# Six more weight blocks prepared during attention, the hash bits first in a score tile, and the instruction order computed anew

## The chip, the cores and the metric

One core of a Trainium2 chip runs the whole program. The metric is the device time of one execution in microseconds (us). The engines are TensorE (PE, with its weight loads as PEld), VectorE (DVE), ScalarE (ACT), GpSimd (POOL) and SyncE (SP), which issues nearly all transfers.

## The reference

Attention with a hash mask, then a gated feed-forward layer:

```python
q_bits = (einsum('bhsd,dk->bhsk', q, proj) > 0)          # 6 bits for each query; k_bits likewise
mask   = q_bucket[:, :, :, None] == k_bucket[:, :, None, :]
scores = where(mask, q @ k.T / sqrt(64), -1e9)           # 4 batches, 8 heads, 768 x 768, head size 64
attn   = exp(scores - max) ; attn /= attn.sum + 1e-9
x      = (attn @ v) as 3072 tokens x 512
out    = (sigmoid(x @ w_gate) * (x @ w_val)) @ w_out     # 512 -> 1536 -> 512
```

The three weight matrices come as 64-bit floats.

## The kernel before

Attention runs over 16 pairs of heads (4 batches, 4 pairs each); a pair has two query groups of three tiles. For a pair, k and q are loaded, turned on PE (tiles `tk`, `tq`), split into a high and a low part (`kh`, `kl`, `qh`, `ql`; every float32 product is three reduced products: low by high, high by low, high by high), and hashed (`hk`, `hq`, with the hash weights `hw`), which gives the bits `kb` and `qb` in bfloat16. `qs..` are q's parts with its halves exchanged by a transfer.

A score tile (`scores`, L713 to L727; 192 of them) is one accumulation of eight matmuls that run in pairs on the upper and lower 64 rows of the array: three pairs of float32 parts (L720) and, last, one bfloat16 pair that adds the hash match (L725). DVE takes the scores out of PSUM with their maximum (L734, `e`), ACT exponentiates (L753), PE turns `e` back in chunks (`tp`, L786), ACT or DVE copies a chunk out (`ef`, L793), and PE multiplies with v (`pv`, L803).

The feed-forward layer has 12 column blocks j. Each block of each matrix (`g`, `v`, `o`: 36 in all) must be made from 64-bit words (`load_w`, L297 to L375): a 512 KB load `raw`, then on DVE `exponent` (L321), `mantissa` (L328), `whole` (L333) and `signed` (L338), on ACT `shifted` (L324) and `high` (L351), on POOL `scaled` (L343) and `low` (L354). There are three classes of blocks. The j below `J1 = 3` are made during attention and stay. The j from 3 to 7 (`J2 = 8`) are made during attention, stored to DRAM (`kept`) and fetched back when attention's buffers are gone (the "switch"). The j from 8 to 11 are loaded and made after the switch, beside the feed-forward work. For six of the eight token units (384 tokens each) the j below 3 are worked off during attention too (`moe_early`: `zg`, `zv`, `zo`); the rest is the late stage (`moe_late`, names ending in `l`), where PE goes through gate (`zg`, 12 matmuls), value (`zv`, 12) and output (`yo`, 9) block by block. Gate products wait in one of two PSUM banks until ACT has made the sigmoid (`sig`, L579).

All instructions are first recorded as tasks. A planner (`Plan.order`) walks through them with written-down durations and buffers and emits them in the order in which its own clock starts them; every engine executes its part strictly in that order. So the written numbers set the order, not the time. `BEGIN` and `LEAVE` are what it charges when PE changes its kind of work, `PATIENCE` how long it puts off a change. A task that two engines could do is listed for both; the second takes it only by a key raised by `SECOND`. A transfer is held to land 2 us plus a share for its bytes after its issue (`dma`, L288). The matmuls `idle` (L273) are stand-ins without use that keep PE at work before data is there.

Of the kernel before, what the change touches and what calls it, by code (L numbers as in the profile page):

```python
# [9 lines left out]
F32 = mybir.dt.float32  # L10
F32R = mybir.dt.float32r
# [8 lines left out]
P = 128  # L20
# [10 lines left out]
SECOND = 3  # L31
# [5 lines left out]
BEGIN = dict(scores=95, turn=36, values=0, all=0)  # L37

PATIENCE = dict(rows=6000, columns=1000, all=1500)
# [130 lines left out]
def lsh_attention_glu_kernel(ctx, tc, q, k, v, proj, w_gate, w_val, w_out, out):  # L170
    nc = tc.nc
# [12 lines left out]
    J2 = 8  # L184
# [22 lines left out]
    praw = const.tile([P, NB], F32, name="praw")  # L207
    nc.scalar.dma_start(praw[0:D], proj)
    nc.scalar.dma_start(praw[D : 2 * D], proj)
# [31 lines left out]
    ALL = range(P // HB)  # L241
    for n, signs, groups in (("q", (1.0, -1.0), ALL), ("k0", (-1.0, 1.0), ALL[::2]), ("k1", (-1.0, 1.0), ALL[1::2])):
        w = const.tile([P, P], F32, name=f"hw{n}", tag="hw")
        nc.vector.memset(w, 0.0)
        for g in groups:
            half = g % 2 if n == "q" else g // 2
            rows = slice(half * D, (half + 1) * D)
            for i, sign in enumerate(signs):
                at_ = g * HB + i * NB
                nc.vector.tensor_scalar_mul(w[rows, at_ : at_ + NB], praw[rows], sign)  # L250
        hi, lo = hw[n] = [const.tile([P, P], F32R, name=f"hw{n}{x}") for x in "hl"]
        nc.scalar.copy(hi, w)
        nc.vector.tensor_sub(lo, w, f(hi))
# [18 lines left out]
    def busy():  # L272
        nc.tensor.matmul(idle, zero[:, :P], zero, start=True, stop=True)  # L273

    W_KEY, W_STEP, W_MORE = 12.0, 2.2, 1.6
    stock = dict(
        one=1, two=3, moe=1, z=2, y=4, kr=2, qr=2, vr=2, h=2, e=12, st=3, su=3, sv=2, rb=2, xs=3,
# [8 lines left out]
    FIRST = -1  # L286

# [9 lines left out]
    def load_w(key, n, j, early, last=None):  # L297
# [69 lines left out]
        c1 = add(key, "dve", 340, mantissa, after=[b1])  # L367
        c2 = add(key, "dve", 610, whole, after=[c1])
        d = add(key, "dve", 610, signed, after=[b2, c2], give=["raw2" if last else "raw1"])
        e = add(key, "pool", 1230, lambda: scaled(nc.gpsimd), after=[d])  # L370
        h = add(key, "act", 520, high, after=[e], take=[] if early or last else ["wk"])
        made[n, j] = add(key, "pool", 1230, lambda: low(nc.gpsimd), after=[h], give=["mid2" if last else "mid1"])
# [231 lines left out]
    def pair(i):  # L604
# [6 lines left out]
        def load(n):  # L611

            if n == "k":
                z[n] = at.tile([P, 2, GT, 2, D], F32, name=f"kr{u}", tag="kr", bufs=stock["kr"])
                from_ = k[b, two].rearrange("h (p c) d -> p h c d", c=NC)
                for h in range(2):
                    for j in range(2):
                        nc.sync.dma_start(z[n][:, h, :, j], from_[:, h, j * GT : (j + 1) * GT])
            else:
                z[n] = at.tile([P, NC, 2, D], F32, name=f"qr{u}", tag="qr", bufs=stock["qr"])  # L620
                from_ = q[b, two].rearrange("h (p c) d -> p h c d", c=NC)
                for m in range(2):
                    nc.sync.dma_start(z[n][:, :, m], from_[:, m])
# [49 lines left out]
        def bits_k(h):  # L673
# [5 lines left out]
            n: add(t0 - 10.72, "sp", 2400, lambda n=n: load(n), tail=4000, take=[n + "r"]) for n in "kq"  # L679
        }  # L680
        needs, last_turn = [], None
        for m, n in enumerate("kq"):
            n_ = t0 - 6 + m
# [8 lines left out]
        for m, n in enumerate("kq"):  # L692
            n_ = t0 - 2.8 + m * 0.6
            a = add(n_, "pe", 6 * MM, lambda n=n: hash_(n), after=[needs[m]], take=["two"])
# [12 lines left out]
    def group(i, g, z, needs, v_here):  # L707
# [162 lines left out]
    for m, (n, j) in enumerate(order):  # L870
        load_w(W_KEY + W_STEP * m + W_MORE * max(0, m - 3 * J1), n, j, j < J1)
# [60 lines left out]
```

## Time and profile before

| what | value |
|---|---|
| median of 3 runs | 1087.22 us (1086.17 to 1087.38) |
| the profiled execution | 1087.43 us |
| its span, first to last instruction | 1085.6 us |
| PE busy | 1057.6 us, 97% of the span |
| DVE, ACT, POOL busy | 569.8, 488.2, 260.6 us |
| TensorE clock granted, mean over the span | 0.997 |

The profile covers one execution. Busy time is the sum of an engine's instructions; a matmul's end is modelled, so PE can be slower than it could be while it counts as busy. Times in timelines count from the start of the span. Attention reaches to about 566 us, the late stage from there to the end. The profiled execution lies 0.2 us from the median, and what is outside its span is 1.8 us.

### The profile page before, as it was taken

The page shows a single profiled execution, that of the slowest core. Times are in us where ns is not written, and L with a number is a line of the kernel's source. Part 1 is how long each engine was busy: PE and PEld are TensorE (multiplying, and loading weights), DVE is VectorE, ACT ScalarE, POOL GpSimd, SP SyncE. Part 2 cuts the span into 40 slices and gives each one's busy share as a digit, 9 for nine tenths or more (in the row PEclk, how much of TensorE's full clock was granted, in tenths as well). Part 3 has the DMA queues.
Part 4 walks back from the last instruction along what each step waited for, and adds up shares of the span by engine and source line. Part 5 has one row for each costly group of instructions (what it writes and reads, how often), then busy time and mean ns, then how long its engine had stood idle before and what let it go on. Part 6 is the DMA issues. An engine that isn't in the chain of part 4 may idle for free.

```text
span 1085.6 us, 20467 instructions
## 1 busy us (share of the span) xinstructions
PE 1057.6 (97%) x8409; PEld 847.1 (78%) x8412; DVE 569.8 (52%) x1200; ACT 488.2 (45%) x878; POOL 260.6 (24%) x235
## 2 busy tenths in 40 slices
PE   9999999999999999999997999999999999999998
PEld 5665567677676776776676889999999999999997
DVE  6899989778778677788730881001120202020201
ACT  2766777667686667775641342112121212121211
POOL 0013243212323122322021672112121212121211
PEclk9999999999999999999999999999999999999999
DMA  8345464444555346424129321002020202020010
GB/s 204 83 130 156 128 180 127 140 119 134 179 142 166 110 128 192 143 70 148 47 83 356 113 82 59 1 1 88 1 88 1 88 1 88 1 74 14 29 30 30
DMA packets 109117, 107.24 MB, mean 99 GB/s; under 512 B 60128, under 2 KB 91872, under 8 KB 109024
## 3 DMA queue, kind: packets, MB, share of 16 engines
q1 hardware_dynamic: 108864, 105.93, 31.7%
q8 instruction: 66, 1.08, 0.4%
q14 instruction: 27, 0.22, 0.1%
q10 hardware_dynamic: 160, 0.00, 0.0%
HBM read 67.64 MB, written 25.69 MB: 86 GB/s over the span
## 4 chain that ended last, share of the span: by engine, by line
PE 79%; DVE 10%; POOL 5%; issue 2%; DMA 2%; ACT 2%; POOLq 0%; DVEq 0%; ACTq 0%
PE pv L803 10%; PE sc L720 8%; PE zv_1l L427 7%; PE zg_1l L427 7%; PE yo_1l L460 7%; PE tp L786 6%; PE zv_0l L427 6%; PE zg_0l L427 5%; PE yo_0l L460 5%; PE zg L427 4%; PE zo L460 3%; PE zv L427 3%; DVE e L734 3%; PE sc L725 2%; PE hk L658 2%
## 5 line engine op out<-in xcount | busy, mean ns | idle before, releaser
L753 ACT ACTIVATE e<-e,st 128x768 f32<-128x768 f32 x192 | 196.3, 1025 | 90.4 <-DVE st L746 90.2
L734 DVE TENSOR_SCALAR_CACHE_REDUCE e<-sc 128x768 f32<-128x768 f32 x192 | 177.8, 952 | 32.0 <-PE sc L725 30.9
L803 PE MATMUL pv<-ef,vr 128*64 128x384 f32 x768 | 140.9, 496 | 0.0
L443 DVE TENSOR_TENSOR gf_1l<-zv_1l,sig 128x384 f32<-128x384 f32 x39 | 21.7, 557 | 208.6 <-PE zv_1l L427 208.6
L786 PEld LDWEIGHTS tp<-ident,e 64*128 64x128 f32 x2304 | 84.7, 139 | 33.2 <-issue 18.5
L793 DVE COPY ef<-tp 128x768 f32<-128x768 f32 x96 | 90.9, 952 | 35.4 <-PE tp L786 33.6
L443 DVE TENSOR_TENSOR gf_0l<-zv_0l,sig 128x384 f32<-128x384 f32 x39 | 21.6, 555 | 162.8 <-PE zv_0l L427 162.8
L786 PE MATMUL tp<-ident,e 64*128 64x64 f32 x2304 | 95.6, 226 | 4.3 <-DVE e L734 1.6
L427 PE MATMUL zg_0l<-xh_0l,wg 128*128 128x384 f32 x312 | 88.1, 342 | 7.3 <-ACT sig L579 7.2
L720 PE MATMUL sc<-kh,ql 64*128 64x384 f32 x192 | 85.9, 447 | 4.8 <-DVE ql L648 2.6
L803 PEld LDWEIGHTS pv<-ef,vr 128*64 128x64 f32 x768 | 48.3, 136 | 52.2 <-issue 48.0
L813 POOL TENSOR_TENSOR xs<-xs,rb 128x384 f32<-128x384 f32 x32 | 32.8, 1025 | 233.8 <-DVE xs L810 174.8
L427 PE MATMUL zv_0l<-xh_0l,wv 128*128 128x384 f32 x312 | 85.9, 336 | 2.5 <-DVE gf_0l L443 2.5
L793 ACT COPY ef<-tp 128x768 f32<-128x768 f32 x96 | 75.1, 793 | 25.9 <-PE tp L786 25.5
L720 PE MATMUL sc<-kh,qsl 64*128 64x384 f32 x192 | 85.9, 448 | 0.8 <-DVE ef L793 0.6
L427 PE MATMUL zg_1l<-xh_1l,wg 128*128 128x384 f32 x312 | 86.4, 337 | 0.0
L427 PE MATMUL zv_1l<-xh_1l,wv 128*128 128x384 f32 x312 | 85.5, 334 | 0.0
L448 POOL TENSOR_TENSOR gl<-gf_1l,gh 128x384 fp32r<-128x384 f32 x39 | 40.5, 1040 | 184.4 <-ACT gh L447 184.4
L460 PE MATMUL yo_0l<-wo,gh 128*128 128x512 f32 x234 | 73.5, 395 | 0.0
L460 PE MATMUL yo_1l<-wo,gh 128*128 128x512 f32 x234 | 73.4, 395 | 0.0
L579 ACT ACTIVATE sig<-zg_1l 128x384 f32<-128x384 f32 x39 | 19.2, 492 | 116.0 <-PE zg_1l L427 116.0
L448 POOL TENSOR_TENSOR gl<-gf_0l,gh 128x384 fp32r<-128x384 f32 x34 | 37.0, 1089 | 135.1 <-ACT gh L447 135.0
(160 smaller groups left out, 2506.7 us busy)
## 6 DMA issues: line engine op xcount, KB each, us to landing
kr<-in_k_dram SPq DMA_DIRECT2D x64, 96.0 KB
qr<-in_q_dram SPq DMA_DIRECT2D x32, 192.0 KB
vr<-in_v_dram SPq DMA_DIRECT2D x16, 384.0 KB
qsh<-qh SPq DMA_DIRECT2D x32, 192.0 KB
qsl<-ql SPq DMA_DIRECT2D x32, 192.0 KB
rb<-rd SPq DMA_DIRECT2D x64, 96.0 KB
xd<-xs SPq DMA_DIRECT2D x32, 192.0 KB
rawg<-in_moe_w_gate_dram SPq DMA_DIRECT2D x12, 512.0 KB
```

What stands on the lines that cost most here:

```text
L427: nc.tensor.matmul(z["acc"][:, :GN], a[:, wc], x[xx][:, c, :], start=(c == 0 and i == 0), stop=(c == KC - 1 and i == 2),)
L443: nc.vector.tensor_mul(z["gf"], z["acc"][:, :GN], sig[:, j])
L448: low = lambda eng: eng.tensor_sub(gl[:, j], z["gf"], f(gh[:, j]))
L460: nc.tensor.matmul(acc, a[:, slot, ts_], w, start=(first and i == 0), stop=(last and i == 2))
L658: nc.tensor.matmul(acc[:, j, :GN], hw[w][a], z[n + x][:, j * GN : (j + 1) * GN], start=m == 0, stop=m == 2,)
L720: nc.tensor.matmul(sc[:, j, :GN], q_[rows, c], z["k" + x][rows, h * GN : (h + 1) * GN], start=(m == 0), stop=False, tile_position=(j * D, 0),)
L734: nc.vector.tensor_scalar(sp(e), gz["sc", t, h][:, :, :GN], -SCALE, None, op0=ALU.mult, op1=ALU.min, accum_out=gz["st", t][:, 0, h : h + 1],)
L753: nc.scalar.activation(e, e, AF.Exp, bias=st[:, 2, h : h + 1], scale=st[:, 1, h : h + 1], accum_out=gz["su"][:, h * GT + t : h * GT + t + 1],)
L786: nc.tensor.transpose(tp[:, r, at_ : at_ + D], gz["e", t, h][rows, c * P : (c + 1) * P], ident[rows, rows], tile_position=(r * D, 0),)
L793: copy(gz["ef", c].rearrange("p (n r d) -> p r n d", r=2, d=D), gz["tp", c][:, :, :GN].rearrange("p r (n d) -> p r n d", d=D),)
L803: nc.tensor.matmul(gz["pv"][rows, :GN], z["v"][:, h, c], gz["ef", c][:, h * GN : (h + 1) * GN], start=(c == 0), stop=(c == NC - 1), tile_p ...
L813: nc.gpsimd.tensor_mul(gz["xs"], gz["xs"], gz["rb"])
```

## The change

Six things are changed.

- `J2` goes from 8 to 10: the six blocks with j = 8 and 9 move from the third class to the second. They are made during attention, stored and fetched back. The spacing of the blocks in attention (`W_MORE`) is made even.
- In `scores` the bfloat16 pair stands first in the accumulation and the float32 pairs follow.
- The first pair's q is loaded through ACT's queue, beside k on SP's; the loads of `proj` follow it there.
- The hash weights are made in one tile of three parts, with one cast and one subtraction, in a task of the planner.
- The planner's numbers are different: larger durations for the weights' steps, 10 us until a fetch or the first late load is held to land (`CROWDED`), `SECOND` 161, a lower `BEGIN` for scores, more `PATIENCE`, two result tiles `xs` where there were three, and later keys for turning and hashing.
- By all this the order of the whole program is made anew.

```diff
-SECOND = 3
+SECOND = 161
...
-BEGIN = dict(scores=95, turn=36, values=0, all=0)
-
-PATIENCE = dict(rows=6000, columns=1000, all=1500)
+BEGIN = dict(scores=60, turn=36, values=0, all=0)
+
+PATIENCE = dict(rows=9000, columns=1000, all=1500)
...
-    J2 = 8
+    J2 = 10
...
+    def load_projection():
+        for half in range(2):
+            nc.scalar.dma_start(praw[half * D : (half + 1) * D, 0], proj)
+
+    def hash_weights():
+        nc.vector.tensor_scalar_mul(praw[:, 1], praw[:, 0], -1.0)
+        nc.vector.tensor_copy(praw[:, 2], praw[:, 0])
...
+        nc.scalar.copy(hi, hw_raw)
+        nc.vector.tensor_sub(lo, hw_raw, f(hi))
...
-        st=3, su=3, sv=2, rb=2, xs=3,
+        st=3, su=3, sv=2, rb=2, xs=2,
...
+    CROWDED = 1600000
...
-        a = dma(key, 524288, load, after=[last or score_tasks[int(key)]], take=["raw2" if last else "raw1"])
-        b1 = add(key, "dve", 340, exponent, after=[a], take=["mid2" if last else "mid1"])
-        b2 = add(key, "act", 620, shifted, after=[b1])
+        a = dma(key, CROWDED if last and j == J2 else 524288, load, after=[last or score_tasks[min(int(key), 90)]], take=["raw2" if last else "raw1"])
+        b1 = add(key, "dve", 440, exponent, after=[a], take=["mid2" if last else "mid1"])
+        b2 = add(key, "act", 700, shifted, after=[b1])
...
+            n: add(t0 - 10.72, "act" if i == 0 and n == "q" else "sp", 1200 if n == "q" else 2400,
+                   lambda n=n: load(n, nc.scalar if i == 0 and n == "q" else nc.sync), tail=4000, take=[n + "r"])
...
-            n_ = t0 - 6 + m
+            n_ = t0 - 4 + m
...
             gz["sc", t, h] = sc = ps2.tile([P, 2, 512], F32, name=f"sc{u}_{t}_{h}", tag="two")
+            for j, rows in enumerate(halves):
+                nc.tensor.matmul(
+                    sc[:, j, :GN], z["qb"][rows, c], z["kb"][rows, h], start=True, stop=False, tile_position=(j * D, 0),
+                )
             for m, (a, x) in enumerate((("l", "h"), ("h", "l"), ("h", "h"))):
...
-                        start=(m == 0), stop=False, tile_position=(j * D, 0),
+                        start=False, stop=(m == 2), tile_position=(j * D, 0),
...
-        load_w(W_KEY + W_STEP * m + W_MORE * max(0, m - 3 * J1), n, j, j < J1)
+        load_w(W_KEY + W_STEP * m, n, j, j < J1)
...
-        made[w] = dma(1e3, 524288, fetch, after=[a, later["switch"]])
+        made[w] = dma(1e3, CROWDED, fetch, after=[a, later["switch"]])
```

On ACT, at the start of the late stage (unit `3_0l`), the program before has these rows; `exg` and `exv` are the first two blocks that are made after the switch, `gh` the split of a gated product.

```order
L498 COPY ob_2_1_8901<-zo_2_1_8878 128x512
L447 CAST gh<-gf_3_0l 128x384
L579 ACTIVATE sig<-zg_3_0l 128x384
L447 CAST gh<-gf_3_0l 128x384
L324 ACTIVATE exg_8985<-exg_8985,ebias 128x512
L579 ACTIVATE sig<-zg_3_0l 128x384
L324 ACTIVATE exv_8994<-exv_8994,ebias 128x512
```

In the changed program the same place on ACT reads as follows.

```order
L509 COPY ob_2_1_8962<-zo_2_1_8946 128x512
L458 CAST gh<-gf_3_0l 128x384
L590 ACTIVATE sig<-zg_3_0l 128x384
...
L458 CAST gh<-gf_3_0l 128x384
L335 ACTIVATE exg_9224<-exg_9224,ebias 128x512
L590 ACTIVATE sig<-zg_3_0l 128x384
L335 ACTIVATE exv_9236<-exv_9236,ebias 128x512
```

Before, two sigmoids of the unit (the other one stands just ahead of these rows) come ahead of the first late block's `exg`; now six do (left out are four more pairs of `sig` and `gh`). On SP, 15 fetches stood ahead of the first late load and now 21 do.

On PE, a score tile of the first pair, before (`sc_0_0_2_1`) and after another score tile:

```order
L720 MATMUL sc_0_0_2_1_479<-kh_0_261,qsl_0_333 128x384
L720 MATMUL sc_0_0_2_1_479<-kh_0_261,ql_0_299 128x384
L720 MATMUL sc_0_0_2_1_479<-kl_0_262,qsh_0_309 128x384
L720 MATMUL sc_0_0_2_1_479<-kl_0_262,qh_0_298 128x384
L720 MATMUL sc_0_0_2_1_479<-kh_0_261,qsh_0_309 128x384
L720 MATMUL sc_0_0_2_1_479<-kh_0_261,qh_0_298 128x384
L725 LDWEIGHTS qb_0_336
L725 MATMUL sc_0_0_2_1_479<-kb_0_306,qb_0_336 128x384
L725 LDWEIGHTS qb_0_336
L725 MATMUL sc_0_0_2_1_479<-kb_0_306,qb_0_336 128x384
```

And the program's first score tile in the changed program.

```order
L282 MATMUL idle<-sig 128x512
L734 LDWEIGHTS qb_0_357
L734 MATMUL sc_0_0_0_0_387<-kb_0_335,qb_0_357 128x384
L734 LDWEIGHTS qb_0_357
L734 MATMUL sc_0_0_0_0_387<-kb_0_335,qb_0_357 128x384
L740 MATMUL sc_0_0_0_0_387<-kh_0_261,ql_0_271 128x384
L740 MATMUL sc_0_0_0_0_387<-kh_0_261,qsl_0_325 128x384
L740 MATMUL sc_0_0_0_0_387<-kl_0_262,qh_0_270 128x384
L740 MATMUL sc_0_0_0_0_387<-kl_0_262,qsh_0_295 128x384
L740 MATMUL sc_0_0_0_0_387<-kh_0_261,qh_0_270 128x384
L740 MATMUL sc_0_0_0_0_387<-kh_0_261,qsh_0_295 128x384
```

The bfloat16 pair, with weights of its own, has moved from the tile's end to its head; the number of matmuls is the same. Counted over the whole order, PE now goes into scores from other work 107 times (102 before) and into turning chunks 123 times (119), and of the 192 `ef` copies DVE has 87 (96 before) and ACT 105. On PE's first instructions 21 stand-ins are followed by the first pair's `tk` and, now at once, its `tq`; before, seven stand-ins lay between the two.

## Rows read from the trace of the kernel before

**Rows 1.** The page's first part: busy time, share of the span, instructions.
```profile
PE 1057.6 (97%) x8409; PEld 847.1 (78%) x8412; DVE 569.8 (52%) x1200; ACT 488.2 (45%) x878; POOL 260.6 (24%) x235
```

**Rows 2.** Windows: stretch, length, busy per engine (instructions), granted clock, DMA share, GB/s.
```profile
0.00:21.60 21.60, 19.46 (x119) 10.85 (x121) 13.25 (x43) 4.58 (x7) 1.35 (x10) 1.00 0.87 215
21.60:160.00 138.40, 131.40 (x1542) 86.48 (x1543) 127.74 (x300) 99.53 (x178) 30.62 (x26) 1.00 0.48 132
160.00:566.00 406.00, 402.60 (x4147) 285.63 (x4146) 311.33 (x691) 272.53 (x472) 96.25 (x86) 1.00 0.43 129
566.00:590.50 24.50, 24.22 (x122) 21.33 (x120) 4.02 (x5) 5.94 (x12) 6.62 (x6) 1.00 0.96 373
590.50:660.40 69.90, 59.89 (x299) 54.30 (x299) 48.82 (x64) 26.13 (x48) 41.10 (x30) 0.95 0.28 96
660.40:1085.60 425.20, 420.01 (x2188) 388.52 (x2186) 64.67 (x98) 79.52 (x163) 84.64 (x80) 1.00 0.11 38
```

**Rows 3.** Timeline of PE after the switch: start, us, work [idle before, releaser].
```profile
589.89 0.63 PE L460 MATMUL yo_0l<-wo,gh 128*128 128x512 f32 x2
596.90 0.69 PE L427 MATMUL zg_0l<-xh_0l,wg 128*128 128x384 f32 x1 [6.38 <-ACT sig L579]
...
600.75 0.34 PE L427 MATMUL zv_0l<-xh_0l,wv 128*128 128x384 f32 x1
...
660.36 0.33 PE L427 MATMUL zg_1l<-xh_1l,wg 128*128 128x384 f32 x1
```

**Rows 4.** Timeline of all engines, 582 to 597 us.
```profile
582.89 0.51 ACT L447 CAST gh<-gf_0l 128x384 fp32r<-128x384 f32 x1 [2.28 <-DVE gf_0l L443]
...
586.24 0.38 SPq L312 DMA_DIRECT2D rawg<-in_moe_w_gate_dram  x1
...
595.28 0.43 DVE L321 TENSOR_SCALAR exg<-rawg 128x512 int32<-128x512 int32 x1 [12.43 <-DMA rawg<-in_moe_w_gate_dram]
...
595.75 0.72 ACT L324 ACTIVATE exg<-exg,ebias 128x512 int32<-128x512 int32 x1 [12.34 <-DVE exg L321]
596.37 0.47 ACT L579 ACTIVATE sig<-zg_0l 128x384 f32<-128x384 f32 x1
```

**Rows 5.** Chain of waits in the late stage: start, us, work.
```profile
673.79 2.10 PE zg_1l L427 x12
...
680.06 2.10 PE zg_1l L427 x12
```

**Rows 6.** Lines by form: busy us, mean ns, then idle before and its releasers.
```profile
L793 DVE COPY ef<-tp 128x768 f32<-128x768 f32 x96 | 90.9, 952 | 35.4 <-PE tp L786 33.6 <-ACT ob L498 1.6
...
L720 PE MATMUL sc<-kh,ql 64*128 64x384 f32 x192 | 85.9, 447 | 4.8 <-DVE ql L648 2.6 <-ACT ef L793 0.9 <-DVE ef L793 0.3
...
L720 PE MATMUL sc<-kl,qh 64*128 64x384 f32 x192 | 63.9, 333 | 0.0
...
L720 PEld LDWEIGHTS sc<-kh,ql 64*128 64x128 f32 x192 | 36.6, 191 | 24.2 <-issue 9.3 <-DVE st L746 5.3 <-ACT ef L793 2.5
...
L725 PEld LDWEIGHTS <-qb 64*128 64x128 bf16 x384 | 18.5, 92 | 30.4 <-issue 29.4
...
L338 DVE SCALAR_TENSOR_TENSOR exv<-rawv,exv 128x512 int32<-128x512 int32 x12 | 10.8, 903 | 0.0
...
L321 DVE TENSOR_SCALAR exv<-rawv 128x512 int32<-128x512 int32 x12 | 7.2, 598 | 3.8 <-POOL wo L354 3.4 <-DMA rawv<-in_moe_w_val_dram 0.4
```

**Rows 7.** Timeline of all engines, 0 to 22 us.
```profile
2.01 6.98 PE L273 MATMUL idle<-sig 128*128 128x512 bf16 x21 [2.01 <-POOL sig L270]
2.82 1.37 SPq L623 DMA_DIRECT2D qr<-in_q_dram  x2
...
8.91 0.59 PE L635 MATMUL tk<-ident,kr 64*128 64x64 f32 x12
...
21.61 0.44 PE L720 MATMUL sc<-kh,ql 64*128 64x384 f32 x1
```

**Rows 8.** Timeline of DVE in the late stage.
```profile
602.88 1.50 DVE L321 TENSOR_SCALAR exo<-rawo 128x512 int32<-128x512 int32 x1 [2.15 <-POOL wg L354]
```

More of the change, by code (lines that the diff above doesn't have):

```diff
@@ L205, in lsh_attention_glu_kernel @@
     make_identity(nc, ident)
-    praw = const.tile([P, NB], F32, name="praw")
-    nc.scalar.dma_start(praw[0:D], proj)
-    nc.scalar.dma_start(praw[D : 2 * D], proj)
+    praw = const.tile([P, 3, NB], F32, name="praw")
     def marked(name, first):
@@ L240, in lsh_attention_glu_kernel @@
     hw = {}
[L241 to L246, printed above, removed]
-            rows = slice(half * D, (half + 1) * D)
[L248 to L253, printed above, removed]
+    hw_raw = const.tile([P, 3, P], F32, name="hw_raw")
+    nc.gpsimd.memset(hw_raw, 0.0)
+    def load_projection():
[4 more added lines that the diff above has]
+        nc.vector.tensor_copy(praw[:, 2], praw[:, 0])
+        for half in range(2):
+            rows = slice(half * D, (half + 1) * D)
+            plus, minus = (praw[rows, m : m + 2].rearrange("p s n -> p (s n)") for m in range(2))
+            to = hw_raw[rows, 0].rearrange("p (a b r) -> p a b r", b=2, r=HB)[:, :, half, : 2 * NB]
+            nc.vector.tensor_copy(to, plus.unsqueeze(1).broadcast_to([D, 2, 2 * NB]))
+            for h in range(2):
+                at_ = (2 * half + h) * HB
+                nc.vector.tensor_copy(hw_raw[rows, 1 + h, at_ : at_ + 2 * NB], minus)
+        hi, lo = (const.tile([P, 3, P], F32R, name=f"hw{x}") for x in "hl")
+        nc.scalar.copy(hi, hw_raw)
+        nc.vector.tensor_sub(lo, hw_raw, f(hi))
+        for m, n in enumerate(("q", "k0", "k1")):
+            hw[n] = hi[:, m], lo[:, m]
     sums = [const.tile([P, 32], F32, name=f"su{m}") for m in range(3)]
@@ L273, in busy @@
         nc.tensor.matmul(idle, zero[:, :P], zero, start=True, stop=True)
[L275 removed]
+    W_KEY, W_STEP = 12.0, 2.2
     stock = dict(
[L277 removed]
+        one=1, two=3, moe=1, z=2, y=4, kr=2, qr=2, vr=2, h=2, e=12, st=3, su=3, sv=2, rb=2, xs=2,
         ef=4, raw1=1, mid1=1, raw2=2, mid2=2, wk=1, xr=1, x=1, ob=3,
@@ L609, in pair, with load @@
         two = slice(2 * hp, 2 * hp + 2)
-        def load(n):
+        def load(n, eng):
             if n == "k":
@@ L678, in pair @@
         here = {
-            n: add(t0 - 10.72, "sp", 2400, lambda n=n: load(n), tail=4000, take=[n + "r"]) for n in "kq"
-        }
+            n: add(t0 - 10.72, "act" if i == 0 and n == "q" else "sp", 1200 if n == "q" else 2400,
+                   lambda n=n: load(n, nc.scalar if i == 0 and n == "q" else nc.sync), tail=4000, take=[n + "r"])
+            for n in "kq"
+        }
+        if i == 0:
+            a = add(t0 - 10, "act", 1200, load_projection, after=[], tail=2500)
+            hw["task"] = add(t0 - 10, "dve", 1500, hash_weights, after=[a])
         needs, last_turn = [], None
         for m, n in enumerate("kq"):
-            n_ = t0 - 6 + m
+            n_ = t0 - 4 + m
             last_turn = add(
@@ L692, in pair @@
         for m, n in enumerate("kq"):
-            n_ = t0 - 2.8 + m * 0.6
-            a = add(n_, "pe", 6 * MM, lambda n=n: hash_(n), after=[needs[m]], take=["two"])
+            n_ = t0 - 2.2 + m * 0.6
+            a = add(n_, "pe", 6 * MM, lambda n=n: hash_(n), after=[needs[m], hw["task"]], take=["two"])
             if n == "k":
```

20 lines of the change are left out of this document (8 added, 12 removed).

## The prediction

> **What bounds the kernel now.** I read the page's busy times first, then the windows, then the timelines of the places where PE stands still. PE is busy 1057.6 us, so all other work matters only where PE waits for it [rows 1]. The windows show where that is [rows 2]. In attention from 21.6 to 160 us PE is idle 138.40 - 131.40 = 7.0 us, with DVE busy 92% of the time; from 160 to 566 us it is idle 3.4 us in 406 and DVE is busy 77%. From 660.4 us to the end it is idle 5.2 us in 425. The one bad stretch is 590.5 to 660.4 us: PE idle 10.0 us of 69.9, and the only one with a granted clock below full, 0.95. So there are two things to gain: that stretch, and PE's own work in attention, which can shrink only if matmuls get cheaper.
>
> The stretch in detail. PE ends an output product at about 590.5 us and starts the next gate product at 596.90, 6.38 us later, released by ACT's sigmoid [rows 3]. ACT had done nothing since 583.4 (582.89 + 0.51): the next instruction in its order, the `shifted` of the first late block, waited for DVE's `exponent` at 595.28, and that waited for a load issued at 586.24, which took 9.0 us [rows 4]. The sigmoid stood right behind and ran at 596.37. It had its input all along; it was queued behind an instruction whose data was not there. Both PSUM banks for gate and value products were full until then, so PE stood.
>
> **Late stage: -10.8 us.** Three costs are in it. First the stall, 6.38. Second the slow gate product behind it: from 596.90 to 600.75 it takes 3.85 us [rows 3] where one takes 2.10 [rows 5], 1.75 more; PE had been without work before, and a clock of 0.95 over 69.9 us is 3.5 us at half clock (1.2 GHz), which says the same. Third, small waits: from 600.75 to 660.36 PE does a value and an output product and eight whole blocks. A block takes 680.06 - 673.79 = 6.27 [rows 5], the first two 6.27 - 2.10 = 4.17, together 54.3; it took 59.6 [rows 3], so 5.3 is lost while twelve blocks are made.
>
> In the new order the first late block stands behind six sigmoids on ACT. When does it get there? Without the stall, PE would begin block j = 3 at 590.5 and end the value product of j = 5 two blocks and 4.2 us later, at 607.2; ACT has split it by about 608. And when is the load there? Six more fetches of 0.524 MB stand ahead of it on SP, 3.15 MB, at the 373 GB/s of that stretch [rows 2] 8.4 us more: 595.3 + 8.4 = 603.7. That is 4 us ahead of ACT, so the stall and the slow gate go, 8.1 us. The blocks of j = 10 are needed by PE seven blocks after j = 3, at 590.5 + 7 x 6.27 = 634, so they have 30 us to be made in; before, twelve were made in the 52 us to 648. Of the small waits I expect half to remain, since half of the blocks do: 2.7 gained. Bounds: 6 (the stall returns in part) and 13.4 (all).
>
> **Score tiles: -4.5 us.** The first pair of a tile, on `ql`, takes 447 ns in the mean and the second, on `kl`, 333: 114 ns in which float32 weights are loaded in the open [rows 6]. Such a load takes 191 ns and the bfloat16 one 92. Where a tile follows another, nothing changes: the cycle of eight matmuls is the same. Where scores begin after other work (107 times in the new order), the load in the open is now the short one, and the long one goes beside the bfloat16 matmuls. At most 191 - 92 = 99 ns are won, 107 x 0.099 = 10.6 us; at least nothing, if the long load then shows one pair later. In proportion to the load's length the exposed part is 114 x 92/191 = 55 ns, so about 59 ns are won; a load of 191 ns hardly fits beside one pair, so I take 50, 5.3 us. Part of the entries lie before 160 us, where PE waits anyway, and I keep 4.5.
>
> **Pieces of work: +1.0 us.** The new order has five more entries into scores and four more into turning. Each pays such an open load, 9 x 0.114 = 1.0. Bounds 0 and 2 (paid on leaving too).
>
> **Start: -0.8 us.** 21 stand-ins run from 2.01 to 9.0 us and the first turn follows at 8.91 [rows 7]; they, not the data, hold it. Now q is turned right behind k, without seven stand-ins between, at most 7 x 6.98/21 = 2.3 us earlier. Against it POOL clears the hash tile before it clears the tile for the stand-ins, and no row shows that clearing; it can cost as much as all of POOL's start, 2.0. I take 0.8 gained of the 21.6 us to the first score tile, ends 2.3 gained and 2.0 lost. That q's issue starts at 0.7 and not at 2.82 [rows 7] is hidden by the stand-ins; the loads of `proj` come behind it on ACT and have until the first hash.
>
> **Waits in attention: -1.0 us.** DVE gives nine `ef` copies to ACT, 9 x 0.952 = 8.6 us [rows 6], counted in the first third. There PE's 7.0 us of waits lie beside a DVE that is 92% busy; I take 2 of them as gained. The six added blocks put four instructions each on DVE, of 0.60 to 0.90 us [rows 6], about 3 us a block, 18 in all, and they are last in the list, so after 160 us: DVE goes from 311 to 329 of 406 us. That fits, but not always at the right moment; I take 1 lost. Ends: 7 gained, 18 lost. The block's work on ACT and POOL has more room [rows 2]; its store and its fetch replace nothing that PE waits for.
>
> One DVE instruction of a block, `exponent`, took 0.43 us in one place [rows 4] and 1.50 in another [rows 8], where POOL was making weights. The Trainium skill, "SBUF - State Buffer", section "Who interferes with whom", says that DVE and GpSimd share a pair of ports that one of them holds for a whole instruction while the other waits, for DVE's fast copies and for those with two inputs in SBUF. By that rule each of the 24 added instructions could wait 1.07 us, 26 us on DVE in a stretch in which it idles 95; the trace agrees with the two durations, and the sum stays as it is as long as that idle time takes it. Where it doesn't is the third rival.
>
> **Sum.** -10.8 - 4.5 + 1.0 - 0.8 - 1.0 = -16.1. From the profiled execution's 1087.43 us that gives 1071.3, and as that lies 0.2 above the median, I forecast 1071 us.
>
> **The rivals.**
> 1. Attention gives nothing: the open load only moves to the second pair, the start and the waits stay. For it: a load of 191 ns is longer than the pair that is to hide it; against it: in a tile behind another tile just that pair hides it. Then 10.8 - 1.0 = 9.8 is gained, 1077.6 us.
> 2. The stall moves: the first late load lands after 608 us. For it: the fetches run at the full rate of the transfers already (share 0.96 [rows 2]), and stores of results lie among them; against it: 4 us of room. If the added fetches take twice as long it lands at 612, ACT blocks the seventh sigmoid, some 5 us of stall and 1.75 of slow clock: 1071 + 6.7 = 1078.
> 3. Slower than before: DVE becomes the bound of the later attention. 18 us of block work and, as the two durations of `exponent` allow (1.50 - 0.43 [rows 4, 8]), 24 x 1.07 = 26 of waiting beside POOL, on the queue in which the score tiles' maximum stands; PE's banks for scores stay full and PE waits. If half of the 44 us comes at such moments, 1071 + 22 = 1093. It decides once PE's idle time from 160 us to the switch exceeds 3.4 + 16.1 = 19.5 us. Against it: DVE idles 406 - 311 = 95 us there [rows 2].
> 4. More than I count: the full 99 ns at each entry (10.6), half of the early waits (3.5), a late stage almost without waits (12), the start 0.8, less 1.0: 25.9, 1061.5 us.
>
> **How the numbers follow.** Forecast 0.50, with its own range of 1066 to 1077; rival 1 0.20; rival 2 0.10; rival 3 0.05; rival 4 0.15. A range of 1063 to 1079 holds the forecast, rivals 1 and 2, and a part of 4. A measurement of this kernel can tell 0.2%, about 2.2 us, from no change. All but rival 3 are faster by more; leaving something for mishaps between, faster 0.92, the same 0.03, slower 0.05.
>
> **What would show it.** Late stage: no idle time of PE over 1 us before the second unit, granted clock 1.00 throughout, and the first `exponent` of a late block without a wait for its load. Score tiles: the first float32 pair no longer longer after a change of work, and PE's busy time in attention some 4 us lower. Start: first score tile near 20.8 us. Attention: PE's idle time to 160 us near 5. I am wrong if the sigmoid again stands behind a late block, or if PE's idle time in attention rises by more than the late stage gives.

## The result, and the profile after

| what | before | after |
|---|---|---|
| median | 1086.70 us (1085.79 to 1087.38, 4 runs) | 1075.22 us (1073.73 to 1077.49, 4 runs) |
| ratio | | 0.9897, 95% interval 0.9875 to 0.9918 |
| the profiled execution, its span | 1087.43, 1085.6 us | 1073.73, 1071.9 us |

The change makes the kernel 11.5 us faster in the medians. The profiled execution of after is the fastest of its four and lies 13.7 us below the one of before; the account below is of these two.

The page's first part, after (to compare with [rows 1]):
```profile
PE 1048.6 (98%) x8409; PEld 849.0 (79%) x8412; DVE 552.2 (52%) x1170; ACT 491.8 (46%) x890; POOL 260.9 (24%) x239
```

The windows of after, in the stretches and columns of [rows 2]:
```profile
0.00:21.60 21.60, 18.74 (x116) 10.67 (x120) 11.94 (x31) 3.29 (x4) 1.70 (x11) 1.00 0.91 212
21.60:160.00 138.40, 130.15 (x1506) 86.31 (x1506) 117.27 (x283) 103.31 (x185) 29.60 (x26) 0.99 0.50 132
160.00:566.00 406.00, 399.29 (x4193) 289.13 (x4189) 327.49 (x717) 281.36 (x492) 112.40 (x98) 1.00 0.48 145
566.00:590.50 24.50, 24.22 (x123) 21.64 (x122) 4.58 (x6) 6.95 (x14) 7.34 (x7) 1.00 0.97 373
590.50:660.40 69.90, 69.74 (x367) 64.77 (x366) 28.68 (x39) 21.20 (x41) 29.42 (x24) 1.00 0.33 118
660.40:1085.60 425.20, 406.48 (x2120) 376.45 (x2118) 62.26 (x94) 75.71 (x155) 80.39 (x76) 1.00 0.10 34
```
Length less PE's busy time is PE's idle time. In the bad stretch, 590.5 to 660.4 us, it falls from 10.0 to 0.16 us, at full clock. In attention it rises, from 7.0 to 8.25 before 160 us and from 3.4 to 6.7 after. The clock of 0.99 before 160 us is one stretch at half clock (1.2 GHz), behind 1.66 us in which PE had waited for a copy `ef`, with PE at work throughout (the window from 127.33 us):
```profile
127.33:130.74 3.41, 3.41 (x20) 2.14 (x18) 3.33 (x8) 0.93 (x2) 1.56 (x2) 0.50 1.03 266
```
Half of these 3.41 us, 1.7, is lost (an estimate from the granted share). The kernel before has no such stretch in attention.

Two places in PE's timeline divide the time: the first gate product of the late stage, 568.01 us before, and that of the second unit of tokens, 660.36 before [rows 3]. After:
```profile
567.99 0.33 PE L438 MATMUL zg_0l<-xh_0l,wg 128*128 128x384 f32 x1
...
646.75 0.33 PE L438 MATMUL zg_1l<-xh_1l,wg 128*128 128x384 f32 x1
```
The first is where it was, the second 13.6 us earlier. So the stretch between them gave the whole gain (92.35 us before, 78.76 after), and attention gave nothing. Attention, from the first score tile to the first late gate, takes 546.4 us before (21.61 to 568.01) and 546.7 after (21.27 to 567.99).

In the late stage, ACT's and DVE's timeline of after shows the place that stood still before [rows 4]:
```profile
592.39 0.38 SPq L323 DMA_DIRECT2D rawg<-in_moe_w_gate_dram  x1
592.71 0.49 ACT L590 ACTIVATE sig<-zg_0l 128x384 f32<-128x384 f32 x1 [3.04 <-PE zg_0l L438]
...
598.98 0.49 ACT L590 ACTIVATE sig<-zg_0l 128x384 f32<-128x384 f32 x1 [3.04 <-PE zg_0l L438]
...
605.24 0.49 ACT L590 ACTIVATE sig<-zg_0l 128x384 f32<-128x384 f32 x1 [3.04 <-PE zg_0l L438]
...
607.84 0.42 DVE L332 TENSOR_SCALAR exg<-rawg 128x512 int32<-128x512 int32 x1
...
608.37 0.72 ACT L335 ACTIVATE exg<-exg,ebias 128x512 int32<-128x512 int32 x1
```
Three sigmoids pass after the load's issue, and the first `exponent` starts at 607.84 with no wait in brackets: DVE gets there after the load has landed.

The first score tile starts at 21.27 us, 0.34 earlier [rows 7]:
```profile
2.36 7.40 PE L282 MATMUL idle<-sig 128*128 128x512 bf16 x21 [2.36 <-POOL sig L279]
...
9.70 0.59 PE L646 MATMUL tk<-ident,kr 64*128 64x64 f32 x12
10.12 0.54 PE L646 MATMUL tq<-ident,qr 64*128 64x64 f32 x12
```
The stand-ins begin 0.35 us later, behind POOL's clearing, and take 7.40 us for 6.98, so the first turn comes 0.79 us later; q follows k at once. Six kernels below keep the old start, and in their traces the first score tile starts between 20.68 and 21.80 us, so a gain of 0.34 cannot be told from none.

### The profile page after: what moved, and what is told of

Same layout as the page of the kernel before. It is cut to its first block, busy times and chain, and to the rows that moved or that the text cites. A ratio compares the mean times of both kernels' runs of the same rounds, so it can differ in the third digit from the quotient of the medians.

```text
span 1071.9 us, 20499 instructions
## 1 busy us (share of the span) xinstructions
PE 1048.6 (98%) x8409; PEld 849.0 (79%) x8412; DVE 552.2 (52%) x1170; ACT 491.8 (46%) x890; POOL 260.9 (24%) x239
## 4 chain that ended last, share of the span: by engine, by line
PE 81%; DVE 7%; ACT 4%; POOL 3%; DMA 2%; issue 2%; SPq 0%; POOLq 0%; DVEq 0%; ACTq 0%
PE pv L819 10%; PE zv_0l L438 8%; PE zv_1l L438 7%; PE sc L740 7%; PE zg_0l L438 7%; PE zg_1l L438 7%; PE yo_0l L471 7%; PE yo_1l L471 7%; PE tp L802 5%; PE zg L438 3%; PE zv L438 3%; PE zo L471 3%; PE sc L734 3%; DVE e L750 2%; ACT e L769 2%
## 5 line engine op out<-in xcount | busy, mean ns | idle before, releaser
L454 DVE TENSOR_TENSOR gf_0l<-zv_0l,sig 128x384 f32<-128x384 f32 x39 | 21.7, 558 | 192.5 <-PE zv_0l L438 192.5
L809 DVE COPY ef<-tp 128x768 f32<-128x768 f32 x87 | 82.0, 950 | 34.8 <-PE tp L802 32.5
L740 PE MATMUL sc<-kh,ql 64*128 64x384 f32 x192 | 90.3, 470 | 0.0
L740 PE MATMUL sc<-kh,qsl 64*128 64x384 f32 x192 | 90.3, 470 | 0.0
L809 ACT COPY ef<-tp 128x768 f32<-128x768 f32 x105 | 81.6, 791 | 11.5 <-PE tp L802 11.1
L459 POOL TENSOR_TENSOR gl<-gf_0l,gh 128x384 fp32r<-128x384 f32 x37 | 39.2, 1059 | 155.8 <-ACT gh L458 155.7
L734 PE MATMUL sc<-kb,qb 64*128 64x384 bf16 x384 | 64.9, 331 | 9.4 <-ACT ef L809 3.3
```

The lines of the kernel that those rows point to most:

```text
L454: nc.vector.tensor_mul(z["gf"], z["acc"][:, :GN], sig[:, j])
L459: low = lambda eng: eng.tensor_sub(gl[:, j], z["gf"], f(gh[:, j]))
L734: nc.tensor.matmul(sc[:, j, :GN], z["qb"][rows, c], z["kb"][rows, h], start=True, stop=False, tile_position=(j * D, 0),)
L740: nc.tensor.matmul(sc[:, j, :GN], q_[rows, c], z["k" + x][rows, h * GN : (h + 1) * GN], start=False, stop=(m == 2), tile_position=(j * D, 0),)
L809: copy(gz["ef", c].rearrange("p (n r d) -> p r n d", r=2, d=D), gz["tp", c][:, :, :GN].rearrange("p r (n d) -> p r n d", d=D),)
```

## The experiments

Twelve kernels. Each ratio is to runs of before on the same chip; the medians of those lie between 1086.82 and 1087.01 us. "Waits of PE" are PE's idle time from 21.6 to 566 us by the windows: 10.4 us before, 15.0 after.

### The bits first, in either order

The kernel before with the bfloat16 pair first and the order kept, by the edit below; then the kernel after with that pair last, by its reverse, its order kept.

```diff
+            for j, rows in enumerate(halves):
+                nc.tensor.matmul(
+                    sc[:, j, :GN], z["qb"][rows, c], z["kb"][rows, h], start=True, stop=False, tile_position=(j * D, 0),
+                )
             for m, (a, x) in enumerate((("l", "h"), ("h", "l"), ("h", "h"))):
...
-            for j, rows in enumerate(halves):
-                nc.tensor.matmul(
-                    sc[:, j, :GN], z["qb"][rows, c], z["kb"][rows, h], start=False, stop=True, tile_position=(j * D, 0),
-                )
```

> The kernel before, with the bfloat16 pair first in a score tile and nothing else; the order of tasks is that of before. Theory A (attention is bound by PE's own work, and what the cheaper tiles save is lost again by the new order's waits): 102 entries into scores at 64 to 102 ns, some 8 us of PE work, of which at least 5 shows: 1079 to 1082 us. Theory B (the end of attention is set by a chain through DVE and ACT, in which PE has room): 1085 to 1087 us, with PE's idle time before the switch grown by as much as its busy time fell.

> The changed kernel with the bfloat16 pair last in a score tile again; its order of tasks is kept. Theory A: 107 entries cost 64 to 102 ns more, 1080 to 1084 us. Theory B: 1074 to 1077 us, as the changed kernel.

Measured: 1080.63 us (ratio 0.9940, 0.9928 to 0.9952), and 1082.28 us (0.9959, 0.9947 to 0.9971). Theory A both times. The last matmul of attention's output products starts at 569.92 and 581.29 us, where it starts at 575.51 both before and after. So the bits first are worth 5.6 us of attention in the old order and 5.8 in the new, and the new order costs attention 5.8 us with the bits last and 5.6 with the bits first. The two cancel in the kernel after. In the medians of the whole time the bits are worth 6.4 us in the old order and some 7 in the new; the profiled execution with the bits last in the new order, 1079.62 us, is one of the fastest of its six (1079.57 to 1083.91).

Where in the tile the time goes is seen in PE's timeline of one single tile that stands between a gate product and turns. In the kernel before:
```profile
227.50 0.44 PE L720 MATMUL sc<-kh,ql 64*128 64x384 f32 x1
...
228.13 0.34 PE L725 MATMUL sc<-kb,qb 64*128 64x384 bf16 x2
228.31 0.28 PE L786 MATMUL tp<-ident,e 64*128 64x64 f32 x4
```
The same tile with the bits first alone:
```profile
225.63 0.34 PE L718 MATMUL sc<-kb,qb 64*128 64x384 bf16 x2
225.67 0.47 PE L724 MATMUL sc<-kh,ql 64*128 64x384 f32 x1
...
226.33 0.35 PE L786 MATMUL tp<-ident,e 64*128 64x64 f32 x6
```
From its start to the next work the tile takes 0.81 us with the bits last and 0.70 with them first. Last, the bfloat16 pair holds its place for 0.18 us (228.13 to 228.31); first, the float32 pair starts 0.04 us behind it. The medians over all tiles say the same: 38 ns to the float32 pair behind it with the bits first alone (192 tiles), 173 ns to a turn behind it before (53 places). The float32 pair then holds its place for 310 ns, where it held it for 284. Over the 102 changes into scores the median saving, from the last matmul ahead of the tiles to the first behind them, is 99 ns, and 63 where turns stand on both sides. The first float32 pair was not slow at entries alone, as the forecast read it: in tiles behind a tile it takes 466 ns, at an entry 437 (medians, before). The bits first leave it slow, in every tile, as the lines by form of after show beside [rows 6]:
```profile
L740 PE MATMUL sc<-kh,ql 64*128 64x384 f32 x192 | 90.3, 470 | 0.0
...
L734 PE MATMUL sc<-kb,qb 64*128 64x384 bf16 x384 | 64.9, 331 | 9.4 <-ACT ef L809 3.3 <-DVE ef L809 3.0 <-DVE e L750 2.4
...
L740 PE MATMUL sc<-kl,qh 64*128 64x384 f32 x192 | 64.3, 335 | 0.0
```

And not all of it arrives. The windows of attention with the bits first alone:
```profile
21.60:160.00 138.40, 130.54 (x1551) 87.84 (x1551) 127.69 (x301) 100.35 (x179) 31.26 (x27) 1.00 0.51 139
160.00:566.00 406.00, 400.97 (x4164) 291.30 (x4161) 311.89 (x694) 273.85 (x476) 100.15 (x88) 1.00 0.44 131
```
The same windows of the kernel after with the bits last:
```profile
21.60:160.00 138.40, 131.60 (x1523) 85.76 (x1520) 116.97 (x284) 104.02 (x185) 30.14 (x26) 1.00 0.50 133
160.00:566.00 406.00, 400.21 (x4146) 282.21 (x4143) 327.91 (x715) 279.56 (x489) 109.92 (x95) 1.00 0.48 144
```
Attention's length (first score tile to first late gate) less PE's waits in that stretch is PE's own work. With the bits first alone the first late gate comes at 562.41 us, and 0.3 of the 12.9 us of waits lie behind it.

| | length | waits of PE | own work |
|---|---|---|---|
| before | 546.4 | 10.4 | 536.0 |
| bits first alone | 540.6 | 12.6 | 528.0 |
| after, bits last | 552.5 | 12.6 | 539.9 |
| after | 546.7 | 15.0 | 531.7 |

The bits first take 8.0 us of work out in the old order and 8.2 in the new, and 2.2 or 2.4 of it come back as waits. In the new order the work taken out is 9.9 us if the 1.7 us at half clock are set aside; of these four traces only after's has such a stretch in attention. The new order adds 3.9 of work with the bits last and 3.7 with the bits first, and 2.2 or 2.4 of waits. Summed by kind of work from each matmul's start to the next one's, idle time taken off, the bits first take 10.3 us (old order) or 9.9 us (new) from the score tiles and add 2.0 or 1.3 to the turns. The new order (bits last, against before) adds 1.6 in score tiles, 0.9 in turns and 1.8 in stand-ins that run after the first score tile (18 in place of 11; the trace of before lacks the record of one), with 0.4 less elsewhere.

What PE waits for changes with the order. For the copies `ef` it waits 2.1 us before, 2.7 with the bits first alone, 8.4 with the bits last in the new order and 10.2 after; for q's low part, q's bits and the sums `su` together, 5.0 before and 0.5 after. ACT's copies stand out. PE's waits for them before (first line) and after, from 21.7 to 566 us (total, times, longest):
```profile
PE sc L720 <- ACT ef L793: 0.9, 3, 0.5
```
```profile
PE sc L734 <- ACT ef L809: 3.3, 9, 0.7
...
PE tp L802 <- ACT ef L809: 2.9, 4, 1.7
```

### The late stage: more blocks early, or the load's tail

Three kernels: before with the large tail alone; after with `J2 = 8`; after with the old tail.

```diff
-        a = dma(key, 524288, load, ...)
+        a = dma(key, 1600000 if last and j == J2 else 524288, load, ...)
...
-        made[w] = dma(1e3, 524288, fetch, ...)
+        made[w] = dma(1e3, 1600000, fetch, ...)
```
```diff
-    J2 = 10
+    J2 = 8
```
```diff
-    CROWDED = 1600000
+    CROWDED = 524288
```

> The kernel before, and the planner holds the fetches and the first late loads (j = 8 here) to land 10 us after their issue; no block is moved. PE's order is that of before. Theory A (the stall is a matter of where ACT's order puts the first late block; the blocks moved are needed only for the small waits): stall and slow gate go, 8.1 us, the small waits of 5.3 us stay: 1078 to 1080 us. Theory B (twelve blocks after the switch are too many; the stall comes back at a later block): 1083 us or more.

> The changed kernel with J2 = 8: the six blocks are made after the switch again, all else is as changed (the planner orders anew). Theory A (the blocks cost attention nothing; they end the small waits): 5 us slower than the changed kernel, 1079 to 1081 us. Theory B (the blocks fill DVE in attention and cost there what they give after the switch): 1073 to 1077 us, with the last score tile some 3 to 5 us earlier.

> The kernel after with the tail of the fetches and of the first late load back at 524288 bytes; J2 stays 10. ACT then reaches the first late block after three sigmoids of the stage, not six. Theory A, the place of that block on ACT is what the stall hangs on: a sigmoid stands behind a `shifted` whose load is still under way, PE idles 4 to 8 us at one place between 585 and 610 us, and the time is 1080 to 1088 us. Theory B, with six late blocks fewer the place no longer matters: no idle time of PE over 1 us, 1073 to 1077 us.

Measured: 1085.96 us (0.9996, 0.9988 to 1.0005), 1085.58 (0.9989, 0.9980 to 0.9997) and 1088.21 (1.0013, 1.0004 to 1.0022). From the first late gate to the second unit's, the three take 91.25, 90.64 and 90.82 us, where before takes 92.35 and after 78.76. Each half alone gives 1 to 2 us, both together 13.6. For the tail alone that is theory B. With the blocks back neither theory came true: both had at most 1081 us. With the old tail it is theory A in kind, with a stall longer than the 4 to 8 us expected and a time just above its range.

With the tail alone the first stall goes, and others come where the twelve late blocks are made too late for PE:
```profile
635.57 0.45 PE L427 MATMUL zg_0l<-xh_0l,wg 128*128 128x384 f32 x1 [1.98 <-POOL wg L354]
639.70 0.44 PE L427 MATMUL zv_0l<-xh_0l,wv 128*128 128x384 f32 x1 [1.74 <-POOL wv L354]
649.44 0.69 PE L427 MATMUL zg_0l<-xh_0l,wg 128*128 128x384 f32 x1 [5.30 <-POOL wg L354]
```
PE now waits for the block itself (POOL's last step, `low`), not for a sigmoid. With the six blocks back in the late stage it is the same:
```profile
636.62 0.44 PE L438 MATMUL zg_0l<-xh_0l,wg 128*128 128x384 f32 x1 [2.48 <-POOL wg L365]
...
650.19 0.69 PE L438 MATMUL zg_0l<-xh_0l,wg 128*128 128x384 f32 x1 [4.98 <-POOL wg L365]
```
With six late blocks but the old tail, the stall of before returns, longer. Six more fetches stand ahead of the load, which is issued 24.3 us after the first late gate where it was 18.2 before, and its first reader comes 10.7 us after the issue instead of 9.0:
```profile
597.39 0.38 SPq L323 DMA_DIRECT2D rawg<-in_moe_w_gate_dram  x1
...
608.07 0.43 DVE L332 TENSOR_SCALAR exg<-rawg 128x512 int32<-128x512 int32 x1 [13.90 <-DMA rawg<-in_moe_w_gate_dram]
...
608.53 0.72 ACT L335 ACTIVATE exg<-exg,ebias 128x512 int32<-128x512 int32 x1 [13.82 <-DVE exg L332]
...
610.31 0.47 ACT L590 ACTIVATE sig<-zg_0l 128x384 f32<-128x384 f32 x1
...
610.84 0.69 PE L438 MATMUL zg_0l<-xh_0l,wg 128*128 128x384 f32 x1 [9.01 <-ACT sig L590]
```
The sigmoid stands behind `shifted`, that behind `exponent`, that behind the load: 9.0 us. The slot on ACT's queue is what the number in the planner moves: `shifted` stands behind three sigmoids of the stage here and behind six in the kernel after. There the load is issued at 592.39 us; at the 10.7 us seen here it lands near 603.1 (an estimate), 4.7 us before `exponent` starts.

### What in the new order costs attention

Moving the blocks back left the start of attention's last output matmul at 575.27 us, so the six blocks are not the cause by themselves. Seven kernels go after it. The first is before with the bits first, `J2 = 10`, the tail and an even step between blocks, without the planner's other numbers and without the new start:

```diff
-    J2 = 8
+    J2 = 10
...
-        load_w(W_KEY + W_STEP * m + W_MORE * max(0, m - 3 * J1), n, j, j < J1)
+        load_w(W_KEY + W_STEP * m, n, j, j < J1)
```

> The kernel before with four edits alone: the bfloat16 pair first, six late blocks (J2 = 10), the large tail for the fetches and the first late load, and an even step between the blocks. The planner's numbers, the keys of turning and hashing, the durations of a block's steps and the start stay as before. Theory A, the attention's loss of some 5.7 us comes from those planner numbers or the start: attention keeps the gain of the bits (its last output product ends near 570), the late stage its 13.6 us, and the time is 1066 to 1069 us. Theory B, any order made anew with six more early blocks loses it: attention ends at 574 to 576 and the time is 1071 to 1076 us.

Measured: 1074.84 us (0.9891, 0.9878 to 0.9903), as after; attention's last output matmul starts at 574.02. Theory B. That mark needs care. Before, after and with the bits first alone, the twelve matmuls of the first late gate stand ahead of it (2.8 us); in this order none do. From the first score tile to that mark, less late gates ahead of it, attention takes 551.1 us before, 545.3 with the bits first alone, 551.4 after and 552.8 here. So this order loses 7.4 us, more than the 5.8 that the bits gain by this measure, though it leaves the planner's numbers alone; 5.9 of it are waits of PE (18.8 for 12.9).

By the same measure every order made anew with the bits first is longer than the old one: blocks back 551.0 us, and of the kernels below the even step 550.8, late blocks and bits with the wide step 550.1, old keys 554.9, old patience and bound 561.4, new patience and bound 554.8, after with the wide step 554.3. That is 4.8 to 16.1 us more than 545.3.

Next, the bits first with the even step alone (eight blocks, old tail); and the kernel with late blocks and bits with a wider step, by this edit:

```diff
-        load_w(W_KEY + W_STEP * m, n, j, j < J1)
+        load_w(W_KEY + W_STEP * m + 0.6 * max(0, m - 3 * J1), n, j, j < J1)
```

> The kernel before with the bfloat16 pair first and the even step of 2.2 turns between the early blocks (before: 3.8 from the tenth block on); eight blocks by each head's stage as before, nothing else changed. Beside it stands the run with the pair first alone, 1080.6 us, attention's end at 569.9. Theory A, blocks made closer together make PE wait for copies that stand behind them on DVE: PE's idle time from 160 to 440 us rises from 3.3 to 6 us or more, attention ends at 573 to 575 and the time is 1084 to 1086 us. Theory B, the step is worth nothing and the six more blocks are what costs: attention ends within 1 us of 569.9, 1080 to 1082 us.

> The run with late blocks and bits only (1074.84 us, attention's end at 574.0), with a step of 2.8 turns from the tenth block on in place of 2.2, so that the thirty blocks reach over nearly the whole attention. Theory A, density is the cost: PE's idle time from 160 to 440 us falls from 7.9 to 4 us, attention ends at 570 to 572 and the time is 1070 to 1072 us, better than the kernel after. Theory B, their number is the cost: attention ends at 574 to 576, 1074 to 1077 us.

Measured: 1090.68 us (1.0034, 1.0021 to 1.0048) and 1072.04 (0.9861, 0.9848 to 0.9875). The windows from 160 to 440 us show where attention lost. With the bits first alone:
```profile
160.00:440.00 280.00, 276.66 (x2871) 202.32 (x2868) 223.53 (x497) 193.65 (x336) 72.84 (x64) 1.00 0.49 144
```
With the even step beside it, blocks and tail as before:
```profile
160.00:440.00 280.00, 274.66 (x2828) 200.11 (x2822) 227.67 (x502) 193.66 (x338) 77.19 (x67) 0.99 0.52 154
```
With late blocks and bits only:
```profile
160.00:440.00 280.00, 272.15 (x2820) 198.62 (x2820) 235.39 (x516) 201.31 (x350) 85.68 (x73) 1.00 0.57 172
```
With the wide step:
```profile
160.00:440.00 280.00, 273.77 (x2834) 199.72 (x2831) 229.36 (x506) 195.51 (x340) 81.98 (x70) 1.00 0.53 157
```
From the first of these to the last, PE waits 3.3, 5.3, 7.9 and 6.2 us while DVE is busy 224, 228, 235 and 229. In these four, more block work in the 280 us goes with more waits. In the new order it does not. There the kernel after and, below it, the same with the wide step have:
```profile
160.00:440.00 280.00, 275.30 (x2869) 199.95 (x2864) 241.32 (x518) 200.48 (x351) 92.14 (x78) 1.00 0.57 172
```
```profile
160.00:440.00 280.00, 274.41 (x2874) 199.07 (x2872) 226.61 (x504) 201.49 (x351) 84.19 (x73) 1.00 0.54 159
```
DVE is busy 15 us less and PE waits more, 5.6 us for 4.7. Since each step also makes a new order, density is not shown to be the cause.

The even step alone costs 5.5 us of attention by the measure above (550.8 for 545.3): 3.1 of waits and some 1.7 at half clock, from 197.96 to 201.38 us. That is theory A in kind, with 5.3 us of waits for 6. Its time lies above both theories, since it loses another 3.7 us in the late stage, where twelve blocks are still to be made and PE's first wait is 4.1 us. The wide step gives back 1.6 us of waits, not the 4 expected, and its second unit begins at 644.84 us, 2.5 earlier than with late blocks and bits only (647.34) and 1.9 earlier than after. In time it is as theory A said.

It is the best version of all: 1072.04 us (1070.75 to 1072.80), ratio 0.9861 against 0.9897 for after, each to its own runs of before; the two intervals just touch. Against late blocks and bits only (0.9878 to 0.9903) it is clearly faster.

The four others change one thing in the new order, or carry one over:

```diff
-            n_ = t0 - 4 + m
+            n_ = t0 - 6 + m
...
-            n_ = t0 - 2.2 + m * 0.6
+            n_ = t0 - 2.8 + m * 0.6
```

> The kernel after with the keys of turning and of hashing as before (6 and 2.8 turns ahead of the scores, not 4 and 2.2). Theory A, turning later is what attention lost: it ends 3 to 6 us earlier than in the kernel after and the time is 1069 to 1072 us. Theory B, the keys are worth nothing: within 1 us of the kernel after, 1074 to 1076 us.

```diff
-BEGIN = dict(scores=60, turn=36, values=0, all=0)
+BEGIN = dict(scores=95, turn=36, values=0, all=0)
-PATIENCE = dict(rows=9000, columns=1000, all=1500)
+PATIENCE = dict(rows=6000, columns=1000, all=1500)
```

> The kernel after with the rows' patience at 6000 and the bound for beginning scores at 95, as before. Theory A, these two cost attention its 5.7 us: attention ends 3 to 6 us earlier than in the kernel after and the time is 1069 to 1072 us. Theory B, they are worth nothing, since the entries into scores and turning rise by a few only (102 runs of score tiles for 107, 80 turns for 76): within 1 us of the kernel after, 1074 to 1076 us.

> The run with late blocks and bits only (1074.84 us) with the rows' patience at 9000 and the bound for beginning scores at 60, as in the kernel after. In the kernel after the old two numbers cost 8 us. Theory A, they are worth that by themselves: attention ends 4 us or more ahead of 574.0 and the time is 1066 to 1071 us. Theory B, they only repair what the other numbers of the new order spoil: the time stays at 1073 to 1077 us.

> The kernel after (1075.22 us, attention's end at 575.5) with a step of 2.8 turns from the tenth block on in place of 2.2. Theory A, density is the cost: attention ends at 571 to 573, 1070 to 1073 us. Theory B, the other numbers of the new order are the cost, since that order loses the same with 24 blocks as with 30: attention ends at 574 to 577, 1074 to 1077 us.

Measured: old keys 1075.73 us (0.9905, 0.9892 to 0.9918), nothing, theory B. Old patience and bound 1083.36 (0.9970, 0.9960 to 0.9981): neither theory, 8 us slower, with waits of PE 19.6 us for 15.0. The new patience and bound on the kernel with late blocks and bits only: 1075.45 (0.9893, 0.9880 to 0.9907), nothing, theory B. The wide step in the new order: 1075.91 (0.9896, 0.9883 to 0.9910), nothing, theory B. So the same numbers are worth 8 us in one order and nothing in another, and none that was put back is by itself the cause of attention's loss; what was tried gives 0 to 3 us. `SECOND`, with the copies that it gives to ACT, the durations of a block's steps, `xs` and the start were not put back one by one. Late blocks and bits only has all of these as before and loses as much, so they are not needed for the loss; its cause stays open.

One pair shows how time is lost in one and the same order. After with the old tail has the same order in attention as after, but in its profiled execution, the slowest of its eleven, a load for an early block lands 3 us later. In the kernel after:
```profile
449.04 0.43 DVE L332 TENSOR_SCALAR exo<-rawo 128x512 int32<-128x512 int32 x1 [1.41 <-DMA rawo<-in_moe_w_out_dram]
```
In the experiment:
```profile
452.07 0.43 DVE L332 TENSOR_SCALAR exo<-rawo 128x512 int32<-128x512 int32 x1 [4.53 <-DMA rawo<-in_moe_w_out_dram]
...
454.08 0.95 DVE L750 TENSOR_SCALAR_CACHE_REDUCE e<-sc 128x768 f32<-128x768 f32 x1
...
455.10 0.90 PE L646 MATMUL tk<-ident,kr 64*128 64x64 f32 x12 [3.09 <-DVE e L750]
```
The maximum `e` stands behind the block's four instructions on DVE, and PE waits 3.1 us for the bank. Then TensorE works at half clock (0.50, 1.2 GHz):
```profile
454.22:461.04 6.82, 5.95 (x52) 3.72 (x52) 5.05 (x11) 4.44 (x9) 2.56 (x2) 0.50 0.21 83
```
The same matmuls that start 0.3 us earlier than in after ahead of this place (308.30 for 308.63) start 5.1 us later behind it (461.86 for 456.81): 5.4 us in all, 3.1 of them the wait. It is the late stage's mechanism, a queue behind a load, in the middle of attention. DVE waits for such loads 0.9 us in attention before, 5.1 after, 5.0 with late blocks and bits only, and 8.5 with late blocks, bits and the wide step, which is the fastest of all; so these waits alone do not rank the kernels. A larger tail for the early blocks' loads too would test what that is worth; it was not tried.

## Why the prediction was right, and where it was not

The forecast was 1071 us in a range of 1063 to 1079; measured 1075.2. Its sum was -16.1 us and the two profiled executions differ by 13.7. Term by term:

| term | predicted | measured in the profiled executions |
|---|---|---|
| late stage | -10.8 | -13.6 |
| score tiles, PE's work | -4.5 | -8.0 |
| pieces of work | +1.0 | +3.7 |
| waits in attention | -1.0 | +4.6 |
| start | -0.8 | -0.3 |
| sum | -16.1 | -13.6 |

That the time fell within the range owes something to luck. Attention with the start was to give 5.3 us and gave nothing; the late stage gave 2.8 more than forecast, and PE's own work 0.8 more, while the waits were 5.6 worse.

**Late stage.** The mechanism was as said: the sigmoid behind a block whose load was not there. The two halves of the change were both needed, which the prediction used without saying it. Mis-sized was the third cost: half of the 5.3 us of small waits was to stay, and none did. The stall, the slow gate and all small waits are 13.4; the upper bound was the value. PE's idle time of 0.16 us and the clock of 1.00 are what was to be seen there. The check on the slow gate was misread: a mean clock of 0.95 over 69.9 us is about 7 us at half clock, not 3.5. The trace has 6.83, from 593.73 to 600.56 us, and in the last 3.66 of them the gate product ran, which gives the same 1.8 us.

**Score tiles.** The gain per entry is 99 ns in the median, where 50 was taken and 99 was the bound. The reason given failed in a part: the first float32 pair is not longer at an entry than elsewhere (437 ns there, 466 in a tile behind a tile), so the 114 ns of the mean were not the open load of an entry, and "no longer longer" did not come true. What a change of work paid was the bfloat16 pair's own place at the tile's end, 0.18 us; ahead of a float32 pair it is 0.04. That the bound of 99 ns was also the value is chance, since it was worked out from the weight loads. PE's busy time in attention fell by 4.6 us, as foreseen, with more taken out and more added than forecast.

**Pieces of work.** Nine entries at 114 ns were counted, 1.0 us. The order's own work rose by nearly four times that. With the bits last, 3.9 us: besides the score tiles (1.6) there are the turns (0.9) and seven more stand-ins (1.8), which a count of entries leaves out. With the bits first, 3.7, of which 1.7 is the half clock at 127 us.

**Waits in attention.** This step failed. Two of the early 7.0 us were to go and one was to come; they became 8.25, and the later 3.4 became 6.7. About half of the rise, 2.2 us, comes with the bits in the old order, 1.3 of it as longer waits for the maximum `e` (3.6 for 2.3). The other half comes with the order. Giving nine `ef` copies to ACT was counted as 2 us gained; in the new order PE waits 6.2 us for ACT's copies where it waited 0.9, and 4.0 for DVE's where it waited 1.2, and this outweighs the 4.5 us of other waits that went. That the handing over is the reason was not tested; blocks closer together on DVE go with more waits in one order and not in the other.

**The rivals.** Attention gave nothing, as the first rival had it, but not for its reason: the load did not move to the second pair, it was the order that took the gain away. The second did not come (`exponent` without a wait at 607.84). The third's condition, more than 19.5 us of idle time from 160 us to the switch, was far off: 6.7.

In the kernel after, DVE's `whole` takes 1.50 us at 608.84 beside POOL's `gl` from 608.55 to 609.80, and 0.69 us at 449.84, where attention runs. The Trainium skill's rule on the shared ports of DVE and GpSimd ("SBUF - State Buffer", section "Who interferes with whom"), for which the prediction kept room, fits these two. The traces also price it. Of a block's DVE instructions in attention, 6 of 96 take over 1 us before and 4 of 120 after, all beside POOL work, together 4.7 and 3.1 us more than the medians of their lines. The third rival's 26 us of such waiting did not come.

## What to carry to other kernels

Where PE is busy 98% of a stretch, what is taken off PE comes back in part as waits for the engines that feed it: here 2.2 of 8.0 us in one order and 2.4 of 8.2 in another. A new order had a price of its own in every case here, 4.8 to 16.1 us of attention, so keep the order and change the instruction first, as the experiment with 5.6 us for one moved pair shows, then change the order. When two orders are compared by a mark in the timeline, look at what work stands ahead of the mark in each. An instruction that waits for a transfer blocks all behind it on its engine; place it by when the load lands, and look for such places wherever blocks are made beside other work, not only where PE stands longest.

## What was not expected of the hardware

From a bfloat16 pair of matmuls to a float32 pair behind it PE takes 0.04 us, and 0.18 to turns behind it at a tile's end. The same eight matmuls so take 0.70 us in one order and 0.81 in the other. And a load of 512 KB in attention that lands 3 us later than in another execution, in the same order, costs PE 5.4 us: 3.1 of waiting, and the rest nearly all at half clock afterwards.
